# One scaling moved to GpSimd, a TensorE order pinned, and a product unit split: an FFT mixer and MLP kernel on one core

## Chip, core, metric

The kernel runs on one core of one Trainium2 chip. The metric is device time in microseconds (us), the median of several runs; smaller is better. A trace of one execution covers the span from the first to the last instruction.

## The reference, cut to what matters

```python
h  = x + irfft2(rfft2(layernorm(x)) * (w_r + 1j * w_i))     # x: [2048, 512]
h2 = h + (gelu(layernorm(layernorm(h)).T @ w1 + b1) @ w2 + b2).T   # w1: [2048, 1376]
```

## The kernel before

Both Fourier transforms are written as matrix products. The kernel has five stages:

1. Front: for each of 16 input tiles, a variance (`bn`, `ag`; for tile 3, sums on ScalarE), its inverse root (`rs`), and a Fourier matrix scaled by it (`fs`). TensorE multiplies tile and scaled matrix (`f1`), and a copy (`ys`) takes the product out of PSUM (`ps` in the traces, the output of every matmul there).
2. Middle, for eight units of four groups: forward products (`f2`), their copy (`cs`), cross products (`x`), the multiply with the filter weights on VectorE (`v`; two ops of 1024 elements for the first unit, one of 2048 for each of the next six, called large below, and two of 1024 for the last, unit 7), inverse products (`g1`), their copy (`pq`).
3. Inverse transform (`g2`, `g3`), residual, second normalisation.
4. and 5. The two layers of the MLP.

Warming matmuls multiply zeros, to keep TensorE busy; experiment 11 shows what its pace does with fewer of them: with 4 at the start, the three behind the first products took 1.46 us in the trace, and with 9, in two traces of the kernel before, 1.46 and 0.82. A scheduler in Python gives each engine its static order from modelled times; lists force parts of it. The lists that the change and the argument touch:

```python
FS_ENG = {0: "act", 3: "act", 7: "act", 9: "dve", 11: "dve", ...}     # all others: GpSimd
FRONT = {
    "act": """rs_0 fs_0 rs_1 s1_3 s2_3 rs_2 rs_3 fs_3 rs_4 ys_0 rs_5 ys_1 ys_3 rs_6 ys_2 fs_7 ...""",
    "pool": """fs_1 bv_3 fs_2 fs_4 fs_5 fs_6 fs_8 fs_10 fs_12""",
    "pe": """f1_0 f1_1 f1_3 f1_2 f1_4 ...""", ...
}
WARM_AFTER = (3, 2, 0, 1, 1, ...)      # warming matmuls (of zeros) behind f1_0, f1_1, ...
V_SPLIT = (7,)                         # unit 7's multiply in two ops
G1_WARM = {(7, 1): 2}                  # two warming matmuls before the last two groups of unit 7
...
# bv_3: a small op on GpSimd; rs_3 on ScalarE takes its result as bias
act(f"rs_{i}", RS[:, i:i + 1], V1[:, i:i + 1], ACT.Abs_reciprocal_sqrt, 1, ..., bias=BV[:, i:i + 1], ...)
```

## Time and profile before

| | |
|---|---|
| time, median of the first 3 runs | 131.5 us (131.47 to 131.62) |
| span of the first profile | 131.3 us, mean granted clock 0.987 |
| time of the very run that was profiled | 133.1 us |
| busy: TensorE, VectorE, ScalarE, GpSimd | 123.3, 70.4, 63.0, 10.8 us |

The page's lines that carry the argument are in the prediction.

### The profile page before, as it was taken

How to read it: one execution, taken by the hardware profiler on the slowest of the kernel's cores; microseconds unless marked ns; L12 is line 12 of the kernel's file. 1: busy time of each engine (PE TensorE's matmuls, PEld its weight loads, DVE VectorE, ACT ScalarE, POOL GpSimd, SP SyncE). 2: the span in 40 equal slices, each digit the busy share in tenths (PEclk: the TensorE clock that was granted, in tenths of full speed). 3: DMA queues.
4: the chain of work that ended last, by engine and by line, in shares of the span. 5: the costliest groups of instructions: out<-in, count | busy, mean ns of one | idle time of the engine just before them, and what ended most of it. 6: DMA issues, size and time to landing. Idle time of an engine off the chain costs nothing.

```text
span 131.3 us, 2029 instructions
## 1 busy us (share of the span) xinstructions
PE 123.3 (94%) x784; PEld 74.8 (57%) x784; DVE 70.4 (54%) x131; ACT 63.0 (48%) x144; POOL 10.8 (8%) x30
## 2 busy tenths in 40 slices
PE   6589989999988989999999999999999999999992
PEld 2134756787866745544444444456666666666681
DVE  0399686999992899999992000000242242332431
ACT  4098996788885999976669922222000000000000
POOL 0067850002100000000000000000000000000000
PEclk9968999999999999999999999999999999999999
DMA  3999999999999999991000000000111211112112
GB/s 72 340 419 380 290 272 293 298 280 279 410 423 419 409 408 409 416 242 42 0 0 0 0 0 0 0 0 5 40 40 40 80 40 66 57 42 80 40 42 81
DMA packets 17481, 22.17 MB, mean 169 GB/s; under 512 B 2784, under 2 KB 13408, under 8 KB 17472
## 3 DMA queue, kind: packets, MB, share of 16 engines
q1 hardware_dynamic: 17184, 21.52, 48.3%
q10 hardware_dynamic: 288, 0.52, 1.6%
q8 instruction: 6, 0.10, 0.3%
q14 instruction: 3, 0.02, 0.1%
HBM read 19.95 MB, written 2.10 MB: 168 GB/s over the span
## 4 chain that ended last, share of the span: by engine, by line
PE 75%; DVE 10%; ACT 8%; DMA 3%; issue 1%
PE ps L556 75%; DVE st L681 5%; DMA X<-in_A_x_dram 3%; DVE V L826 3%; ACT Y L574 3%; ACT EO L574 2%; ACT JK L574 1%; ACT rs L574 1%; DVE Y L743 1%; ACT PQ L574 1%; DVE mv L682 1%; PE ps L647 0%; DVE OUT L934 0%; DVE FS L659 0%; ACT FS L574 0%
## 5 line engine op out<-in xcount | busy, mean ns | idle before, releaser
L556 PE MATMUL ps<-HH,W 128*128 128x512 bf16 (+1 forms) x176 | 40.5, 379 | 0.0
L556 PE MATMUL ps<-GT,W 128*128 128x512 bf16 (+3 forms) x187 | 38.3, 367 | 0.0
L934 DVE SCALAR_TENSOR_TENSOR OUT<-ps,B2f,H 128x512 bf16<-128x512 f32 (+1 forms) x17 | 12.2, 719 | 46.3 <-PE ps L556 46.3
L556 PEld LDWEIGHTS ps<-GT,W 128*128 128x128 bf16 (+1 forms) x187 | 26.3, 145 | 12.0
L556 PEld LDWEIGHTS ps<-HH,W 128*128 128x128 bf16 (+1 forms) x176 | 17.4, 100 | 19.4 <-issue 0.6
L826 DVE TENSOR_TENSOR V<-ps,W 128x2048 bf16<-128x2048 f32 (+1 forms) x8 | 15.8, 2020 | 0.3
L574 ACT ACTIVATE JK<-H,nm 128x512 bf16<-128x512 bf16 x16 | 11.6, 725 | 3.9 <-DVE H L901 3.7
L574 ACT ACTIVATE GT<-ps,B1f 128x512 bf16<-128x512 f32 (+1 forms) x11 | 7.0, 692 | 12.7 <-PE ps L556 12.7
L681 DVE BATCH_NORM_STATS2 st<-X 128x6 f32<-128x512 bf16 x15 | 9.8, 665 | 4.2 <-DMA X<-in_A_x_dram 4.2
L901 DVE TENSOR_TENSOR H<-ps,TT 128x512 bf16<-128x512 f32 x16 | 10.9, 684 | 0.1
L647 PE MATMUL ps<-ZT 128*128 128x512 bf16 x21 | 8.0, 500 | 3.1 <-DVE st L681 1.4
L574 ACT ACTIVATE PQ<-ps 128x512 bf16<-128x512 f32 (+1 forms) x16 | 9.2, 588 | 3.6 <-PE ps L556 3.5
L556 PE MATMUL ps<-EM,V 128*128 128x128 bf16 x128 | 9.8, 219 | 0.4 <-ACT PQ L574 0.3
L574 ACT ACTIVATE EO<-ps 128x512 bf16<-128x512 f32 x16 | 9.3, 599 | 0.9 <-PE ps L556 0.9
L556 PE MATMUL ps<-FS,X 128*128 128x256 bf16 x64 | 9.0, 288 | 0.7 <-ACT FS L574 0.5
L574 ACT ACTIVATE CS<-ps 128x512 bf16<-128x512 f32 (+1 forms) x16 | 8.9, 588 | 1.2 <-PE ps L556 1.2
L556 PEld LDWEIGHTS ps<-EM,V 128*128 128x128 bf16 x128 | 7.9, 98 | 2.3 <-issue 1.1
L556 PE MATMUL ps<-EM,Y 128*128 128x256 bf16 x64 | 8.8, 273 | 0.4 <-DVE Y L743 0.4
L556 PE MATMUL ps<-EM,PQ 128*128 128x256 bf16 x64 | 8.6, 273 | 0.5 <-ACT PQ L574 0.5
L574 ACT ACTIVATE Y<-ps 128x512 bf16<-128x512 f32 (+1 forms) x15 | 8.1, 566 | 0.8 <-PE ps L556 0.8
L556 PEld LDWEIGHTS ps<-FS,X 128*128 128x128 bf16 x64 | 6.1, 102 | 3.7 <-ACT FS L574 1.0
L659 POOL TENSOR_SCALAR FS<-FP,rs 128x256 bf16<-128x256 bf16 x8 | 7.5, 940 | 8.1 <-ACT rs L574 7.9
(38 smaller groups left out, 78.5 us busy)
## 6 DMA issues: line engine op xcount, KB each, us to landing
W<-in_B_w_dram SPq DMA_DIRECT2D x8, 688.0 KB, 9.8
W<-in_B_w_dram SPq DMA_DIRECT2D x10, 512.0 KB, 16.7
out_dram<-OUT SPq DMA_DIRECT2D x15, 128.0 KB, 1.7
W<-in_A_w_r_dram SPq DMA_DIRECT2D x4, 257.0 KB, 4.8
W<-in_A_w_i_dram SPq DMA_DIRECT2D x4, 257.0 KB, 5.5
X<-in_A_x_dram SPq DMA_DIRECT2D x4, 256.0 KB, 5.4
X<-in_A_x_dram SPq DMA_DIRECT2D x2, 512.0 KB, 6.7
W<-in_A_w_r_dram SPq DMA_DIRECT2D x4, 192.8 KB, 3.5
```

Of the source, the lines that this page charges most:

```text
L556: return K.op(name, "pe", lambda eng, bank: eng.matmul(outf(bank), lhsT, rhs, start=start, stop=stop), ins=ins or [lhsT, rhs], occ=occ, la ...
L574: return eng.activation(dst, s, func, **kw)
L647: return K.op(name, "pe", lambda eng, bank: eng.matmul(ps[:, bank, :], ZT[:, 0:NP], ZT[:, :], start=True, stop=True), ins=[ZT[:, :]], occ= ...
L659: dve(f"fs_{i}", lambda eng, bank: eng.tensor_scalar(FS[:, i, :, :], FP[:, i, :, :], rs, None, op0=ALU.mult), [FP[:, i, :, :], rs], [FS[:, ...
L681: dve(f"bn_{i}", lambda eng, bank, i=i, x=x: eng.bn_stats(ST[:, i, 0:6], x), [x], [ST[:, i, 0:6]], 512, prio=25)
L682: dve(f"ag_{i}", lambda eng, bank, i=i: eng.bn_aggr(MV[:, i, :], ST[:, i, 0:6]), [ST[:, i, 0:6]], [MV[:, i, :]], 20, prio=32)
L743: dve(name, lambda eng, bank: eng.tensor_copy(dst, src(bank)), [], [dst], n, unit=unit, prio=28, last=last)
L826: return eng.tensor_tensor(vout, s, win, ALU.mult)
L901: return eng.tensor_tensor(hs.rearrange("p (h d) -> p h d", h=2), e, tt[:, :, :], ALU.add)
L934: dve(f"fin{s2}_{c0}", lambda eng, bank, dst=dst, bia=bia, hs=hs, n=c1 - c0: eng.scalar_tensor_tensor(dst, ps[:, bank, 0:n], bia, hs, op0= ...
```

## The change

Its intent: relieve ScalarE, the busiest engine of the second part of the front (7.24 of 7.40 us), of one scaling; pin a TensorE order that helps VectorE's chain of multiplies to start; and shorten what stands between VectorE's last multiply and the inverse transform.

```diff
-FS_ENG = {0: "act", 3: "act", 7: "act", ...
+FS_ENG = {3: "act", 7: "act", ...
-    "act": """rs_0 fs_0 rs_1 s1_3 s2_3 rs_2 rs_3 ...
+    "act": """rs_0 s1_3 rs_1 s2_3 rs_2 rs_3 ...
-    "pool": """fs_1 bv_3 fs_2 ...
+    "pool": """fs_0 fs_1 bv_3 fs_2 ...
-V_SPLIT = (7,)
+V_PARTS = {7: ((0, 2), (2, 1), (3, 1))}       # unit 7 in ops of 2, 1 and 1 groups
-G1_WARM = {(7, 1): 2}
+G1_WARM = {(7, 1): 1}
+def fill_order():        # the order of f2 and x at the entry, forced on TensorE
+    ...
+    return f2(0) + f2(1) + f2(2)[:3] + x(0) + f2(2)[3:] + f2(3) + x(1) + [n for g in range(4, 16) for n in f2(g)]
 ...                      # the code that emits v_7 takes its parts from V_PARTS
```

More of the change, by code (lines that the diff above doesn't have):

```diff
@@ L496 @@
 RS_GROUPS = ((0,), (1,), (2,), (4,), (5,), (6, 7), (8,), (9, 10), (11, 12), (13,), (14, 15))
-FS_ENG = {0: "act", 3: "act", 7: "act", 9: "dve", 11: "dve", 13: "dve", 14: "dve", 15: "dve"}
+FS_ENG = {3: "act", 7: "act", 9: "dve", 11: "dve", 13: "dve", 14: "dve", 15: "dve"}
 Y_EVAC = (("single", ("act",), ("act",)),) * 6 + (("single", ("dve",), ("act",)), ("single", ("dve",), ("act", "act")))
@@ L502 @@
         tl_0 th_0 h_0 tl_1 th_1 h_1 hh_0""",
-    "act": """rs_0 fs_0 rs_1 s1_3 s2_3 rs_2 rs_3 fs_3 rs_4 ys_0 rs_5 ys_1 ys_3 rs_6 ys_2 fs_7 rs_8 ys_4 ys_5 rs_9 ys_7 rs_11 ys_6 ys_8
+    "act": """rs_0 s1_3 rs_1 s2_3 rs_2 rs_3 fs_3 rs_4 ys_0 rs_5 ys_1 ys_3 rs_6 ys_2 fs_7 rs_8 ys_4 ys_5 rs_9 ys_7 rs_11 ys_6 ys_8
         rs_13 ys_9 ys_10 rs_14 ys_11 ys_13 yh_150 yh_151
         eo_0 eo_1 eo_2 eo_3 eo_4 q_0 r2_0 eo_5""",
-    "pool": """fs_1 bv_3 fs_2 fs_4 fs_5 fs_6 fs_8 fs_10 fs_12""",
+    "pool": """fs_0 fs_1 bv_3 fs_2 fs_4 fs_5 fs_6 fs_8 fs_10 fs_12""",
     "pe": """f1_0 f1_1 f1_3 f1_2 f1_4 f1_5 f1_7 f1_6 f1_8 f1_9 f1_10 f1_11 f1_12 f1_13 f1_14 f1_15""",
@@ L511, with f2, x @@
 WARM_AFTER = (3, 2, 0, 1, 1, 0, 0, 1, 0, 0, 0, 0, 0, 0, 0, 0)
-V_SPLIT = (7,)
+V_PARTS = {7: ((0, 2), (2, 1), (3, 1))}
 LAST_WARM = 7
 MM1B_FROM = {5: 54000.0, 6: 62000.0}
-G1_WARM = {(7, 1): 2}
+G1_WARM = {(7, 1): 1}
+def fill_order():
+    def f2(g):
+        return [f"f2_{g}_{k}" for k in (("00", "10", "01", "11") if g == 0 else ("00", "01", "10", "11"))]
+    def x(g):
+        return [f"x_{g}_{c}{r}" for c in range(2) for r in range(2)]
+    return f2(0) + f2(1) + f2(2)[:3] + x(0) + f2(2)[3:] + f2(3) + x(1) + [n for g in range(4, 16) for n in f2(g)]
 def build_kernel(nc, A_x, A_w_r, A_w_i, B_w1, B_b1, B_w2, B_b2, out):
@@ L525, in build_kernel @@
     K.forced = {e: FRONT[e].split() for e in ("dve", "act", "pool")}
-    K.forced["pe"] = [f"{n}_{b}{h}" for n in FRONT["pe"].split() for b in range(2) for h in "ab"]
+    K.forced["pe"] = [f"{n}_{b}{h}" for n in FRONT["pe"].split() for b in range(2) for h in "ab"] + fill_order()
     T = K.setup_memory(memory_layout(), es)
@@ L815, in stage_x, with tt @@
         g0 = 4 * u
-        nh = 2 if u in V_SPLIT else 1
-        ng = 4 // nh
-        for h in range(nh):
-            wt = W[:, g0 + h * ng:g0 + h * ng + ng, :, :]
+        for gl, ng in V_PARTS.get(u, ((0, 4),)):
+            wt = W[:, g0 + gl:g0 + gl + ng, :, :]
             win = bass.AP(wt.tensor, wt.offset + 1, [list(wt.ap[0]), [LW, 2 * ng], [1, 2], [2, NP]])
-            vout = V[:, g0 + h * ng:g0 + h * ng + ng, :, :].rearrange("p g w l -> p (g w l)")
-            def tt(eng, bank, h=h, win=win, vout=vout):
-                s = psf[:, bank * 512 + h * 512:bank * 512 + h * 512 + 256 * ng]
+            vout = V[:, g0 + gl:g0 + gl + ng, :, :].rearrange("p g w l -> p (g w l)")
+            def tt(eng, bank, gl=gl, ng=ng, win=win, vout=vout):
+                s = psf[:, bank * 512 + gl * 256:bank * 512 + gl * 256 + 256 * ng]
                 s = bass.AP(s.tensor, s.offset, [list(s.ap[0]), [256, ng], [0, 2], [1, 256]])
                 return eng.tensor_tensor(vout, s, win, ALU.mult)
-            K.op(f"v_{u}_{h}", "dve", tt, ins=[wt], outs=[vout], occ=50.0 + 2130.0 / nh, lat=170.0 + 2130.0 / nh, unit=unit, pr=True,
-                 last=h == nh - 1, prio=11, after=wload[u])
+            K.op(f"v_{u}_{gl}", "dve", tt, ins=[wt], outs=[vout], occ=50.0 + 532.5 * ng, lat=170.0 + 532.5 * ng, unit=unit, pr=True,
+                 last=gl + ng == 4, prio=11, after=wload[u])
     lastg1 = [None]
```

## The prediction

> **What bounds the kernel now.** I read the windows view first, cut where the work changes: 5.3 to 12.2 us (statistics and first products), to 19.6 (rest of the forward transform), to 23.9 (entry of the middle stage), to 39.9 (middle stage), to 41.2 (its exit), to 47.8 (inverse transform and second normalisation), then both layers of the MLP. Columns: stretch, length, busy us and instruction count of TensorE, weight load, VectorE, ScalarE and GpSimd, granted clock, DMA share, GB/s.
>
> ```profile
> 5.30:12.20 6.90, 5.46 (x24) 2.33 (x25) 6.80 (x20) 5.21 (x16) 4.00 (x5) 0.75 1.03 406
> 12.20:19.60 7.40, 6.63 (x51) 4.41 (x52) 5.84 (x19) 7.24 (x20) 5.20 (x12) 1.00 1.10 286
> 19.60:23.90 4.30, 4.29 (x44) 2.90 (x45) 2.78 (x3) 2.71 (x6) 0.00 (x0) 1.00 1.08 294
> 23.90:39.90 16.00, 15.47 (x209) 12.29 (x206) 15.81 (x8) 13.37 (x26) 1.28 (x7) 1.00 1.05 343
> 39.90:41.20 1.30, 0.82 (x11) 0.53 (x9) 0.44 (x2) 0.65 (x2) 0.00 (x0) 1.00 1.06 436
> 47.80:131.30 83.50, 80.94 (x396) 46.78 (x396) 33.77 (x70) 26.58 (x63) 0.00 (x0) 1.00 0.22 76
> ```
>
> The reader is to see a different limit in each row: ScalarE from 12.2 to 19.6 us (7.24 of 7.40), VectorE's eight large multiplies from 23.9 to 39.9 (15.81 of 16.00), and from 47.8 on TensorE, which nothing in the change touches. The change can only bring the start of the inverse transform (41.2 us) forward or put it back, and what it gains there arrives nearly whole at the end.
>
> Second, the timeline of the first stage (start, length, engine, line, operation, count, idle before and who ended it):
>
> ```profile
> 6.60 0.51 ACT L574 ACTIVATE FS<-FP,rs 128x256 bf16<-128x256 bf16 x1
> 7.17 0.87 PE L556 MATMUL ps<-FS,X 128*128 128x256 bf16 x4 [0.48 <-ACT FS L574]
> 7.46 0.93 POOL L659 TENSOR_SCALAR FS<-FP,rs 128x256 bf16<-128x256 bf16 x1 [6.62 <-ACT rs L574]
> 8.10 1.46 PE L647 MATMUL ps<-ZT 128*128 128x512 bf16 x3
> 9.35 1.06 PE L556 MATMUL ps<-FS,X 128*128 128x256 bf16 x4
> 10.47 0.74 PE L647 MATMUL ps<-ZT 128*128 128x512 bf16 x2
> 11.05 1.04 PE L556 MATMUL ps<-FS,X 128*128 128x256 bf16 x8
> 11.69 0.60 ACT L574 ACTIVATE Y<-ps 128x512 bf16<-128x512 f32 x1 [0.64 <-PE ps L556]
> 14.72 0.29 DVE L659 TENSOR_SCALAR FS<-FP,rs 128x256 bf16<-128x256 bf16 x1 [1.17 <-ACT rs L574]
> ```
>
> TensorE stands in one unbroken queue from the first scaled matrix (7.17 us) to the third product (11.05 us), warming matmuls between; ScalarE waits 0.64 us for that product, and from there it hardly stops until 18.2 us. VectorE then waits 1.17 us for ScalarE's ninth statistic. So the first scaling, done at 7.11 us, looks critical by way of TensorE's queue, though the chain of waits itself runs through VectorE's statistics at this place.
>
> Third, the timeline of VectorE in the middle and of the exit:
>
> ```profile
> 21.43 2.36 DVE L811 TENSOR_TENSOR V<-ps,W 128x1024 bf16<-128x1024 f32 x2 [0.76 <-PE ps L556]
> 23.93 2.29 DVE L826 TENSOR_TENSOR V<-ps,W 128x2048 bf16<-128x2048 f32 x1
> ...
> 39.68 0.59 PE L647 MATMUL ps<-ZT 128*128 128x512 bf16 x2
> 40.11 0.61 PE L556 MATMUL ps<-EM,V 128*128 128x128 bf16 x8
> 40.54 0.42 DVE L857 CAST PQ<-ps 128x256 bf16<-128x256 f32 x1 [0.62 <-PE ps L556]
> 40.76 0.38 ACT L574 ACTIVATE PQ<-ps 128x256 bf16<-128x256 f32 x1 [0.59 <-PE ps L556]
> 41.20 0.39 PE L556 MATMUL ps<-EM,PQ 128*128 128x256 bf16 x2 [0.48 <-ACT PQ L574]
> ```
>
> The first two multiplies end at 23.79 us and the next starts at 23.93; and at the exit two warming matmuls stand in front of the last eight products, although their last input was ready at 39.91 us.
>
> [...] granted clock 0.50 from 7.38 to 10.78 us (TensorE busy only 1.49 of the 3.40 us before), and 1.00 afterwards. [...] the trace shows 1.22 us at 1024 and 2.28 at 2048 elements[...], so I use it for 512: 0.69 us, an estimate. [...] the 128x256 scaling takes 0.93 us on GpSimd, 0.28 on VectorE and 0.51 on ScalarE. [...]
>
> **The change, part by part.**
>
> First scaling on GpSimd. ScalarE loses one instruction of 0.51 us, some 0.40 of its pace. GpSimd is idle, and would start 0.09 us after the statistic ends at 6.57 (the gap before its scaling at 7.46 in the trace), end at 7.59, and hand over in some 0.08: the first product at 7.67 instead of 7.17, 0.50 later. Behind it the queue is serial. With the clock at half until 10.79 as now: four products 1.06 (the row at 9.35), handover 0.06, three warming matmuls 1.25 (8.10 to 9.35), four products 1.0, handover 0.05, two warming matmuls now at full clock 0.44. Sum 7.67 + 3.86 = 11.5 against 11.05: the third product is some 0.44 late, and so are its copy on ScalarE and all behind it. The 0.40 us that ScalarE saves lie before its wait of 0.64 us, so they only lengthen that wait. What speaks against charging all of it: the clock's switch may move in favour of the later start, and there is relief in the order of ScalarE's early statistics. I charge +0.25, a choice between 0.05 and 0.44.
>
> TensorE order at the entry. As traced the order is already the one now fixed, but for one product: the fourth of group 3 stands behind the four of the second cross unit (it starts at 22.09, they at 21.77). Fixed, it starts at some 21.67; its copy on ScalarE starts right after the one before, at 22.06 instead of 22.41, and the cross products of the next unit, held by that copy until 23.18, could start at 22.75, when the first multiply has freed their bank. The third multiply then starts when VectorE is free, about 23.71 instead of 23.93: −0.22. The whole VectorE chain has four such holes, 0.22, 0.13, 0.15 and 0.12 (starts against the pace of 2.20 us for 2048 elements), 0.62 together; the later three lie behind an order that the change doesn't fix, so I count none of them.
>
> Last unit in three ops, one warming matmul fewer. VectorE's last op of 1024 elements (1.21 us) becomes two of 0.69 that overlap by 0.08: it ends at 39.99 instead of 39.91, so +0.08 there. But the four products of the third quarter need only the first of them (39.38) and start behind the single warming matmul, at 39.68 + 0.22 = 39.90 instead of 40.11; the last four follow at 40.12, their input being there. Last product of the stage: 40.50 instead of 40.72; the copy and the inverse transform follow: −0.21.
>
> Later stages: nothing is edited there, but the order is chosen from modelled times, so it may come out otherwise. TensorE's only holes there are some 0.20 at 46.6 and 0.49 at 47.8 us: ±0.3, mean 0.
>
> Sum: +0.25 − 0.22 − 0.21 = −0.18, so 131.5 − 0.2 = **131.3 us**.
>
> **The rivals.** The first: the front pays the full +0.44, because TensorE's queue there really is serial. For it: ScalarE's wait of 0.64 us named TensorE, and no idle time of 0.1 us on ScalarE behind it. Then 131.5, and up to 131.9 if the middle gives its gain back. The second: the front hides the later start altogether, because another input holds the third product or the clock comes up in time; for it, that the chain of waits names VectorE's statistics up to 12.17 us; against, that VectorE sits idle 1.17 us afterwards. Then 131.5 − 0.43 = 131.1, and 130.7 if the new order closes the other holes of VectorE. The third: the multiply that starts earlier becomes bound by TensorE (its next cross products ended at 26.21, 0.06 before the multiply that needs them), so that the 0.22 is lost one unit later and the gain is the exit's alone: 131.5 + 0.25 − 0.21 = 131.5.
>
> **Range and chances.** The rivals span 130.7 to 131.9, and 2% is 2.6 us, more than all holes named. I take 130.7 to 131.8 for 8 in 10, and faster 0.02, same 0.97, slower 0.01.
>
> **What would show it right or wrong.** In the changed profile: the first product near 7.7, the third near 11.3 to 11.5 and the first product of the middle stage between 19.6 and 20.1 us; the first 2048-element multiply no more than 0.05 us after the one before ends; from the last multiply's end to the inverse transform 1.0 us instead of 1.29; and from there to the end the same 90.1 us. Wrong if the third product comes no later (then the front was not bound by that queue), if the middle grows holes elsewhere, or if the last stretch changes by over 0.3 us.

The marks stand where statements on the clock, on the time of a multiply and on GpSimd's rate were cut, which no trace of this case shows; the traced figures beside them remain. No term of the sum is cut: +0.25 − 0.22 − 0.21 = −0.18. The 0.69 us for 512 elements had been worked out with a formula; a straight line through the two traced times gives the same, 1.22 − (2.28 − 1.22)/2 = 0.69, an estimate. That the clock comes up earlier or later was a guess; the traces show only that its time differs: full clock is recorded from 10.79 us on in the first profile and from 9.61 in that of experiment 11, and in the second profile of before three warming matmuls take 0.82 us from 7.18 on, against 1.46 in the stretch at 0.50. The handover from GpSimd to TensorE, put at some 0.08 us, was 0.06 in the changed kernel's trace (6.94 to 7.00).

## The result

The changed kernel takes 131.65 us (131.60 to 131.73, 4 runs), the kernel before 131.55 us in the same rounds. The ratio is 1.0009, with a 95% interval from 0.9991 to 1.0026: the same, if anything 0.1 us slower. A ratio here and below is the mean time of one kernel's fast runs over that of the other's of the same rounds, so not quite the ratio of the medians quoted.

The profile of the changed kernel has a span of 129.9 us and a clock of 1.00. Against the first profile of before (131.3 us) this looks like a gain of 1.4 us, which the times deny. So before was profiled again, unchanged, in the first experiment: 129.8 us and 1.00. In both of these traces the first statistic starts at 4.67 us, so they can be laid side by side. The windows view was cut, in each kernel, at the first statistic, the first product of the middle, the first multiply, the first multiply of unit 7, the first product of the inverse transform, and the end. The columns are as in the prediction.

Kernel before, profiled again:

```profile
4.67:18.11 13.44, 11.16 (x76) 6.38 (x76) 12.65 (x37) 12.26 (x34) 9.18 (x17) 1.00 1.05 345
18.11:19.93 1.82, 1.82 (x17) 1.28 (x18) 0.43 (x2) 1.02 (x3) 0.00 (x0) 1.00 1.01 271
19.93:36.05 16.12, 16.05 (x209) 12.41 (x207) 15.82 (x8) 13.38 (x26) 1.28 (x7) 1.00 1.08 322
36.05:39.70 3.65, 2.50 (x34) 2.02 (x35) 2.78 (x3) 2.32 (x5) 0.00 (x0) 1.00 1.02 418
39.70:129.79 90.09, 86.59 (x435) 51.19 (x443) 38.49 (x81) 32.37 (x76) 0.00 (x0) 1.00 0.29 106
```

Changed kernel:

```profile
4.67:18.38 13.71, 11.03 (x75) 6.36 (x75) 12.64 (x37) 11.89 (x33) 10.06 (x18) 1.00 1.07 344
18.38:20.20 1.82, 1.82 (x17) 1.28 (x18) 0.43 (x1) 1.02 (x3) 0.00 (x0) 1.00 1.08 275
20.20:36.33 16.13, 16.05 (x209) 12.34 (x207) 15.82 (x8) 13.38 (x26) 1.27 (x7) 1.00 1.06 312
36.33:39.76 3.43, 2.50 (x33) 1.92 (x34) 2.84 (x4) 2.31 (x5) 0.00 (x0) 1.00 1.03 427
39.76:129.86 90.10, 87.18 (x443) 51.26 (x443) 38.50 (x81) 32.35 (x76) 0.00 (x0) 1.00 0.29 107
```

The second number of each row is the stretch's length. The front is 0.27 us longer, the entry and the middle are level, the exit is 0.22 us shorter, and the rest is level. The sum is about +0.06 us, which agrees with the +0.1 us of the times. Differences of 0.1 us in the first and the last stretch are no chance: in the nine traces that have the scaling on ScalarE (the first profile and that of experiment 11 left out) the front takes 13.43 or 13.44 us, and from the inverse transform to the end all fourteen traces take 90.08 to 90.15 us. (The 435 and 443 matmuls of the last row are no change: the first profile of before has 443 as well, in the same order as the changed kernel; some records are missing.)

Where the front lost its 0.27 us is seen in the timeline between the first statistic and the statistic of tile 3. Before, profiled again (ScalarE's second statistic, GpSimd's second scaling, GpSimd's bias op, ScalarE's statistic of tile 3):

```profile
6.41 0.30 ACT L574 ACTIVATE rs<-mv,eps 128x1 f32<-128x1 f32 x1
...
6.80 0.93 POOL L659 TENSOR_SCALAR FS<-FP,rs 128x256 bf16<-128x256 bf16 x1 [5.96 <-ACT rs L574]
...
7.72 0.31 POOL L667 TENSOR_SCALAR bv<-sm 128x1 f32<-128x1 f32 x1
...
8.13 0.29 ACT L574 ACTIVATE rs<-v,bv 128x1 f32<-128x1 f32 x1
```

Changed (GpSimd's first and second scaling merged into one line, ScalarE's sum of tile 3, its second statistic, the bias op, the statistic of tile 3):

```profile
6.01 2.01 POOL L668 TENSOR_SCALAR FS<-FP,rs 128x256 bf16<-128x256 bf16 x2 [5.17 <-ACT rs L583]
6.08 0.63 ACT L583 ACTIVATE JK<-X 128x512 bf16<-128x512 bf16 x1 [0.17 <-DMA X<-in_A_x_dram]
...
6.71 0.28 ACT L583 ACTIVATE rs<-mv,eps 128x1 f32<-128x1 f32 x1
...
7.99 0.32 POOL L676 TENSOR_SCALAR bv<-sm 128x1 f32<-128x1 f32 x1
...
8.41 0.29 ACT L583 ACTIVATE rs<-v,bv 128x1 f32<-128x1 f32 x1 [0.45 <-POOL bv L676]
```

GpSimd's two scalings end at 8.02 instead of 7.73, so the bias op starts at 7.99 instead of 7.72. ScalarE now stands idle 0.45 us for it, and takes up the statistic of tile 3 at 8.41 instead of 8.13. This is the 0.28 us: from there to the copy of the third product ScalarE shows no idle time in either kernel, and each instruction of it is late by the same amount. GpSimd's second scaling is late for two reasons. It queues behind the first one (6.01 + 0.93 = 6.94, 0.14 later than its old start at 6.80). And its input, the second statistic, ends at 6.99 instead of 6.71, because the sum ahead of it waited for its tile and took 0.63 us.

In the middle, VectorE's timeline before (profiled again), the six multiplies of 2048 elements and the two of unit 7 as one merged line:

```profile
22.43 15.98 DVE L826 TENSOR_TENSOR V<-ps,W 128x2048 bf16<-128x2048 f32 x8
```

and changed:

```profile
20.20 2.36 DVE L820 TENSOR_TENSOR V<-ps,W 128x1024 bf16<-128x1024 f32 x2 [0.76 <-PE ps L565]
22.59 2.29 DVE L833 TENSOR_TENSOR V<-ps,W 128x2048 bf16<-128x2048 f32 x1
25.05 13.70 DVE L833 TENSOR_TENSOR V<-ps,W 128x2048 bf16<-128x2048 f32 x8 [0.17 <-PE ps L565]
```

In the changed kernel the first of the large ones starts 0.03 us after the two before it end (22.56), as the pinned order wanted. But the next one waits 0.17 us for TensorE. Counted from the first multiply, it starts 4.85 us later in the changed kernel (25.05 − 20.20) and 4.84 us later in the one before (24.77 − 19.93, from the unmerged trace). The gain at the first is lost at the second.

At the exit of the changed kernel, the last eight inverse products, their two copies:

```profile
38.68 0.61 PE L565 MATMUL ps<-EM,V 128*128 128x128 bf16 x8
39.10 0.42 DVE L864 CAST PQ<-ps 128x256 bf16<-128x256 f32 x1 [0.34 <-PE ps L565]
39.32 0.38 ACT L583 ACTIVATE PQ<-ps 128x256 bf16<-128x256 f32 x1 [0.38 <-PE ps L565]
```

They start 2.35 us after the first multiply of unit 7 (36.33), against 2.56 in the kernel before (profiled again), whose first multiply of unit 7 starts at 36.05:

```profile
38.61 0.61 PE L556 MATMUL ps<-EM,V 128*128 128x128 bf16 x8
```

### The profile page after: what moved, and what is told of

Its sections match the earlier page's. It is cut to its first block, busy times and chain, and to the rows that moved or that the text cites. A ratio compares the mean times of both kernels' runs of the same rounds, so it can differ in the third digit from the quotient of the medians.

```text
span 129.9 us, 2029 instructions
## 1 busy us (share of the span) xinstructions
PE 122.1 (94%) x783; PEld 74.3 (57%) x783; DVE 70.5 (54%) x132; ACT 62.4 (48%) x143; POOL 11.6 (9%) x31
## 4 chain that ended last, share of the span: by engine, by line
PE 76%; DVE 10%; ACT 8%; DMA 3%; issue 1%
PE ps L565 76%; DVE st L690 4%; DVE V L833 3%; DMA X<-in_A_x_dram 3%; ACT Y L583 3%; ACT EO L583 2%; ACT JK L583 1%; ACT rs L583 1%; DVE Y L752 1%; ACT PQ L583 1%; DVE mv L691 1%; DVE OUT L941 0%; DVE FS L668 0%; ACT FS L583 0%; PE ps L656 0%
## 5 line engine op out<-in xcount | busy, mean ns | idle before, releaser
L833 DVE TENSOR_TENSOR V<-ps,W 128x2048 bf16<-128x2048 f32 (+2 forms) x9 | 15.9, 1811 | 0.3 <-PE ps L565 0.2
L656 PE MATMUL ps<-ZT 128*128 128x512 bf16 x20 | 7.2, 470 | 2.3 <-DVE ZT L603 1.2
L668 POOL TENSOR_SCALAR FS<-FP,rs 128x256 bf16<-128x256 bf16 x9 | 8.4, 935 | 6.0 <-ACT rs L583 5.7
```

The lines of the kernel that those rows point to most:

```text
L656: return K.op(name, "pe", lambda eng, bank: eng.matmul(ps[:, bank, :], ZT[:, 0:NP], ZT[:, :], start=True, stop=True), ins=[ZT[:, :]], occ= ...
L668: dve(f"fs_{i}", lambda eng, bank: eng.tensor_scalar(FS[:, i, :, :], FP[:, i, :, :], rs, None, op0=ALU.mult), [FP[:, i, :, :], rs], [FS[:, ...
L833: return eng.tensor_tensor(vout, s, win, ALU.mult)
```

## The experiments

There were twelve runs, one of the kernel before and eleven of edited kernels, all with correct results. Unless said otherwise each was timed in five rounds against the kernel before.

### 1. The kernel before, profiled again

No edit; the question is the state of the first profile.

> The kernel before, unchanged, profiled again. Theory A: the first profile of before (span 131.3 us, clock 0.987, its own time 133.1 us) fell in an execution with a half-clock window that the timed runs (131.5 us) do not have; then the new profile has clock 1.00 and a span of 129.8 +- 0.2 us, 1.8 us under the time as in the four runs of the changed kernel (129.9 under 131.65), and its first scaled product starts about 1.85 us after the first statistic starts. Rival B: the half-clock window belongs to the kernel before; then clock 0.987 and 131.3 us again. Time ratio 1.000 in both.

It took 131.58 us against 131.60 (ratio 1.0001, 0.9989 to 1.0013), with a span of 129.8 us and a clock of 1.00. The first scaled product started 1.84 us after the first statistic. Theory A holds: the first profile was of a slower execution. Compared to this one, in the first profile the first statistic is 0.66 us later (5.33 against 4.67) and the first product of the middle another 0.84 us later after it (14.28 against 13.44), with half clock in between (0.50 from 7.38 to 10.78 us); 0.66 + 0.84 is the whole 1.5 us.

### 2. The scaling on GpSimd alone

```diff
 # kernel before
-FS_ENG = {0: "act", 3: "act", ...          +FS_ENG = {3: "act", ...
-"act": rs_0 fs_0 rs_1 s1_3 s2_3 ...        +"act": rs_0 s1_3 rs_1 s2_3 ...
-"pool": fs_1 bv_3 fs_2 ...                 +"pool": fs_0 fs_1 bv_3 fs_2 ...
```

> The kernel before with the first scaling moved to GpSimd and nothing else. Theory A (the scaling holds GpSimd 0.93 us, so GpSimd's second scaling and the small bias op behind it come late, ScalarE's third statistic waits for that op, and ScalarE is busy without a break from there): +0.3 us, 131.85. Rival B (the front hides it, and the changed kernel is level because middle and exit gave nothing): +-0.05 us, 131.55.

It took 131.91 us against 131.60 (ratio 1.0035, 1.0011 to 1.0060). One of its six runs, at 132.98 us with a clock of 0.987, is in the ratio; the other five lie from 131.81 to 131.96. Theory A holds. In its trace ScalarE waits 0.32 us for the bias op; the statistic of tile 3 starts 3.60 us after the first statistic, against 3.46 before and 3.74 in the changed kernel. It is only 0.14 late here because the input tile of ScalarE's sum had landed earlier relative to the first statistic (1.25 us after it, against 1.39 in the trace of the changed kernel), so that ScalarE's second statistic was done just when GpSimd came free of its first scaling: here GpSimd's own queue accounts for the whole delay, and the later statistic adds nothing to it. The front of this trace is 0.14 us longer than before (13.58 against 13.44 us), not 0.31; how the 0.31 us of the median comes about in the other runs stays open. No run has the scaling on GpSimd with ScalarE's old order of `rs_1` and `s1_3`, so the two edits of this step are told apart by the traces alone.

### 3. The changed kernel with the scaling back on ScalarE

```diff
 # changed kernel: the three lines of experiment 2, reversed
```

> The changed kernel with the first scaling back on ScalarE; TensorE order, three-op unit and single warming matmul stay. Theory A: -0.2 us against before, 131.35, about 0.3 under the changed kernel. Rival B: as the changed kernel, 131.65.

131.35 us against 131.60 (ratio 0.9985, 0.9973 to 0.9997). In its trace the front takes 13.44 us, as before, and the whole from the first statistic on 124.90 us, against 125.12 before and 125.19 in the changed kernel. The rest of the change is worth 0.2 us, and the scaling lost it.

### 4. The bias op first

```diff
 # changed kernel
-"pool": fs_0 fs_1 bv_3 fs_2 ...
+"pool": fs_0 bv_3 fs_1 fs_2 ...
```

> The changed kernel, GpSimd's small bias op put in front of its second scaling (order: first scaling, bias op, second scaling). Theory A (the late bias op is the cost): ScalarE's statistic of tile 3 starts some 0.25 us earlier, 131.35 to 131.4. Rival C (the late first product on TensorE's queue is the cost, as predicted): the first product is as late as in the changed kernel and the time stays at 131.65.

The median is 131.38 us against 131.60. One of six runs took 132.88 us; with it the ratio is 0.9999 (0.9966 to 1.0033), which alone says nothing. The other five lie from 131.19 to 131.40, under ten of before's eleven (131.37 to 131.80). The trace decides between the theories. The bias op, the statistic of tile 3 and the third product (the first four of these eight):

```profile
6.94 0.31 POOL L676 TENSOR_SCALAR bv<-sm 128x1 f32<-128x1 f32 x1
7.77 0.28 ACT L583 ACTIVATE rs<-v,bv 128x1 f32<-128x1 f32 x1
9.33 1.04 PE L565 MATMUL ps<-FS,X 128*128 128x256 bf16 x8
```

The first statistic starts at 4.53 us in this trace. The third product on TensorE starts 4.80 us after the first statistic, even later than in the changed kernel (4.76) and 0.45 later than before. Yet the statistic of tile 3 starts after 3.24 us, and the first product of the middle after 13.36, 0.35 earlier than in the changed kernel and 0.08 earlier than before. So the late bias op cost the time and the late products did not.

But of these 0.35 us only 0.15 reaches the end: from the first statistic on the whole takes 125.04 us, against 125.19 in the changed kernel and 124.90 in experiment 3. In this trace the last of the filter weights landed at 29.43 us, and the fourth large multiply, ready at about 28.96, started at 29.45.

### 5. The exit alone

```diff
 # kernel before
-V_SPLIT = (7,)              +V_PARTS = {7: ((0, 2), (2, 1), (3, 1))}
-G1_WARM = {(7, 1): 2}       +G1_WARM = {(7, 1): 1}
```

> The kernel before with only the exit changed (last unit in three ops, one warming matmul fewer). Theory A (the whole gain is the exit's, the TensorE order gives nothing because the next multiply waits for its own cross products instead): the same as with the order kept, -0.22 us against before, 131.35; in the trace, from the first multiply's start to the inverse transform 19.56 us instead of 19.77. Rival D (the order gives 0.1 to 0.2 of it): 131.45 to 131.55.

131.39 us against 131.57 (ratio 0.9984, 0.9971 to 0.9998). Experiment 3, which has the pinned order as well, had 0.9985. In the traces both take the same 124.90 us from the first statistic to the end. The pinned order, as the change has it, is worth nothing, and experiment 2 plus this one (+0.31 − 0.18) makes +0.13 us, near the +0.10 of the whole change.

### 6 and 7. The two exit edits apart

```diff
 # kernel of experiment 3; run 6                # run 7
-G1_WARM = {(7, 1): 1}                          -V_PARTS = {7: ((0, 2), (2, 1), (3, 1))}
+G1_WARM = {(7, 1): 2}                          +V_PARTS = {7: ((0, 2), (2, 2))}
```

> The changed kernel with the first scaling back on ScalarE and with two warming matmuls at the exit as before; the last unit stays in three ops. Theory A (the two exit edits are worth something only together: the second warming matmul pushes the last eight products back by 0.22 us, whatever the split): level with before, 131.6. Rival F (the split alone is the gain): 131.35.

> The changed kernel with the first scaling back on ScalarE and the last unit in two ops as before; one warming matmul. Theory A: the last eight products then wait for the second op's end, 0.07 us before their start with two warming matmuls: 0.05 to 0.1 us under before, 131.5. Rival G (the missing warming matmul alone is the gain): 131.35.

Three ops with two warming matmuls: 131.73 us against 131.57 (ratio 1.0008, 0.9995 to 1.0020). Two ops with one: 131.44 (0.9986, 0.9974 to 0.9999). The cleaner measure is the stretch from the first multiply of unit 7 to the inverse transform: 3.64 us before (3.65 above, where the edges were rounded), 3.63 with the split alone, 3.50 with one warming matmul alone, 3.43 with both. The split alone gives nothing, as expected: the second warming matmul covers it. The missing matmul alone gives 0.14, twice what was expected; I had taken a longer handover from VectorE to TensorE than the 0.05 us that the trace shows there. The split adds its 0.07 only then.

In both of these traces the fourth large multiply was held by the filter weights. VectorE's timeline of run 7, from the fourth multiply on:

```profile
29.60 8.95 DVE L833 TENSOR_TENSOR V<-ps,W 128x2048 bf16<-128x2048 f32 x5 [0.35 <-DMA W<-in_A_w_i_dram]
```

The weights landed at 29.58 us here, and at 28.35 us in the second profile of before, where the multiply was ready at 29.18. So with a faster front or middle this load is the next bound, in some executions and not in others.

### 8. The order pinned one step further

```diff
 # kernel of experiment 3
-... + x(1) + [n for g in range(4, 16) for n in f2(g)]
+... + x(1) + f2(4) + f2(5)[:3] + x(2) + x(3) + f2(5)[3:] + g1(0..3) + x(4) + x(5) + [n for g in range(6, 16) for n in f2(g)]
```

> The changed kernel with the first scaling back on ScalarE, and TensorE's order fixed one step further: the last product of forward group 5 ahead of the first inverse products, and the cross products of the third unit ahead of forward groups 6 and 7. Theory A (the third multiply's cross products end 0.2 us too late, which ate what the fixed order gave): the hole in front of the second 2048-element multiply closes and the chain ends 0.2 us earlier, 131.15. Rival E (VectorE's chain is then held further on, by the last block of filter weights landing at 28.9 us or later, or by later cross products): 131.35.

A miss: 132.36 us against 131.57 (ratio 1.0055, 1.0042 to 1.0069). The hole that it aimed at did close: the second large multiply started 19.85 us after the first statistic instead of 20.11. But a new hole of 1.08 us stands in front of the sixth, waiting for TensorE. The scheduler, fed with other modelled times, had put the cross products of that unit behind inverse and forward products.

### 9. TensorE's whole middle order written out

```diff
 # kernel of experiment 3
-+ fill_order()
++ MID      # the order of experiment 3 as a list, with: f2_5_11 behind x_3; x_4, x_5 ahead of f2_6, f2_7;
+           # f2_10_11, f2_12_11 with their groups; g1_15_11, g1_19_11 ahead of x_10, x_12
```

> As the run with the order fixed further, but with TensorE's whole order of the middle stage written out, so that nothing later is rearranged: that of the changed kernel with the last product of forward groups 5, 10 and 12 kept with its group, the third unit's cross products ahead of forward groups 6 and 7, and the last inverse product of units 3 and 4 ahead of the cross products. Theory A (VectorE's holes are TensorE's order): the holes before the second, fifth and seventh large multiply close, 0.25 + 0.15 + 0.13: 130.9 with scaling on ScalarE, and exit as changed. Theory A with rival E (the fourth multiply cannot start before the last filter weights land, 28.4 to 29.6 us in the runs so far): some 0.25 of that is lost in front of the fourth, 131.1. Rival: 131.35, nothing.

131.29 us against 131.68 (ratio 0.9966, 0.9954 to 0.9978). This is the fastest kernel, faster than before by some 0.4 us and than the changed one. Its runs and those of the changed kernel were not in the same rounds; by their ratios to before it takes 0.9957 of the changed kernel's time (0.9966 / 1.0009). VectorE's timeline from the first large multiply on:

```profile
22.37 8.89 DVE L851 TENSOR_TENSOR V<-ps,W 128x2048 bf16<-128x2048 f32 x4
31.64 6.82 DVE L851 TENSOR_TENSOR V<-ps,W 128x2048 bf16<-128x2048 f32 x5 [0.38 <-PE ps L583]
```

The first four now run without a break, but the fifth waits 0.38 us. In the trace the gain over experiment 3 is therefore only 0.08 us (124.82 against 124.90 from the first statistic to the end). How much of the 0.4 us in the times is more than that and the exit's 0.22 is not settled; the intervals are as wide as the difference.

### 10. The filter weights in halves

```diff
 # kernel of experiment 9
-for ch, (u0, u1) in enumerate(((0, 1), (1, 4), (4, 8))):
+for ch, (u0, u1) in enumerate(((0, 1), (1, 4), (4, 6), (6, 8))):
```

> The previous kernel, with the last block of filter weights (units 4 to 7) loaded as two blocks (4 and 5, 6 and 7), each with its own wait: eight more transfers of half the size. Rival E holds if the fourth multiply then starts right behind the third and the time falls 0.1 to 0.3 us below the previous kernel, 130.85 to 131.0. If the weights are not what holds it: the same time; if the extra issues (0.65 us each) delay the later loads: slower.

In the first profile four issues of such a weight block took 2.60 us, 0.65 each.

131.52 us, against 131.29 for experiment 9 in the same rounds (ratio to before 0.9977, 0.9962 to 0.9992). It is inconclusive as a test: in neither trace was the fourth multiply held, and both take 124.82 us from the first statistic to the end. The fourth multiply started right behind the third at 29.33 us while the last weights landed only at 30.82, so it no longer waited for the whole load; but nothing shows what this is worth in an execution where the undivided load would be late. Nor is the last rival of the expectation excluded, that the added transfers cost time: the median is 0.23 us worse, though the intervals of the two ratios overlap.

### 11. Fewer warming matmuls at the start

Timed in three rounds.

```diff
 # kernel before
-N_WARM = 9
+N_WARM = 4
```

> The kernel before with 4 instead of 9 warming matmuls at the very start[...]. Theory A (the 1.2 to 1.6 us by which the first profile of before was longer than its timed runs are one half-clock window over the first products): every run has a mean clock of 0.98 to 0.99, the third product is some 1.4 us later after the first statistic, 132.8 to 133.1 us. Rival: the long profile was long for its late inputs alone (0.66 us later) and the clock costs nothing: 131.6.

The mark stands for a length of time that TensorE would have to be busy; no run shows such a length, and it is cut.

132.95 us against 131.68 (ratio 1.0087, 1.0058 to 1.0116; runs from 132.30 to 133.43). TensorE's timeline, the three warming matmuls behind the first products:

```profile
8.11 1.46 PE L647 MATMUL ps<-ZT 128*128 128x512 bf16 x3
```

The three take 1.46 us, as in the first profile of before, and 0.82 in the second one (start at 7.18). In the first profile the clock is recorded at 0.50 over these three, so the same pace is taken for half clock here. The third product starts 1.06 us later after the first statistic (5.41 against 4.35), and the first product of the middle 0.54 us later (13.98 against 13.44). The other 0.51 us of this trace's longer span are a later first statistic (5.18 against 4.67). ScalarE waits 0.43 us for the third product here, a wait that apart from this trace only the first profile of before shows (0.64 us). The rival, that the clock costs nothing, falls; of theory A the cause holds and the size does not. Read so, the clock costs 0.5 us here, not 1.2 to 1.6. And the mean granted clock reads 1.00, though the pace shows half: the clock's record in this trace has its first entry at 9.61 us, and what went before is counted as full (1.00 for 5.0 to 9.6 us in the windows view, the three matmuls in it). The 1.27 us by which the median is longer is thus explained for 0.5 us only; whether the later input is chance, and why the times of this kernel spread over 1.1 us, is not settled.

### 12. Cross products further ahead

```diff
 # kernel of experiment 9: in MID, x_10 and x_11 ahead of g1_14; x_12 and x_13 ahead of g1_18
```

> The kernel with the pinned TensorE order, with the cross products of units 5 and 6 moved ahead of eight inverse products each. Theory A: there the hole of 0.38 us in front of the fifth large multiply came from cross products that ended at 31.57 us, 0.4 us after VectorE was free; moved ahead they end at about 31.1 and the hole closes: 0.3 to 0.4 us under the pinned kernel, 0.75 us under before, 130.9. Rival: a later multiply waits for its cross products, or for a copy on ScalarE, instead: level with the pinned kernel, 0.4 us under before.

131.89 us against 131.76 (ratio 1.0005, 0.9961 to 1.0048); a run of 132.83, and two such of before, make the interval wide. The rival's mechanism holds, and it costs more than the rival said. The fifth large multiply now starts without a hole, 26.46 us after the first statistic instead of 26.92. But the inverse products put back delay their copy on ScalarE, this delays the last forward copies, and the multiply of unit 7 waits 0.54 us for its cross products. From the first statistic to the end it is 125.16 us, against 124.82 in experiment 9, so 0.34 us worse where the rival said level.

## Why the prediction was right, and where its steps were not

The time of 131.65 us lies in the range of 130.7 to 131.8, and "same" had 0.97 of the chances. That is little merit: 2% is 2.6 us, and the range was wide enough to hold both a gain and a loss. The sum, −0.18, should have been about +0.1, so the sign was wrong, and its steps fared differently.

**What bounds the kernel now.** That gains and losses before the inverse transform arrive at the end held: 90.09 and 90.10 us in the two traces. But the front was read from an execution in half clock, in which TensorE's queue stood in front of ScalarE. The two traces of the kernel before differ in it: the clock is 0.50 from 7.38 to 10.78 us in the first and full there in the second. I quoted the fall and did not ask whether the timed runs have it, although the 133.1 us of the profiled run were there to be read.

**First scaling on GpSimd, charged +0.25 by way of TensorE's queue.** The size came out right (0.27 in the changed kernel's trace; in experiment 2 0.31 in the times and 0.14 in its trace), the mechanism was not, so the size was luck. The third product did come later, by 0.41 us counted from the first statistic (4.76 against 4.35), as the working said (0.44 there, though its own terms add up to 11.53 us, 0.48 late). But in the usual state it is not what ScalarE waits for. The 0.28 us arise from the bias op that stands behind two scalings in GpSimd's queue, and experiment 4 shows it: with the bias op ahead the products are later still and the front is faster than before. The step "they only lengthen that wait" failed, as there is no such wait in the usual state. The prediction's signs could not tell: it took a third product that comes later as a sign of being right, and the product did come later, but nothing waited for it. The second rival, that the front hides the scaling altogether, is refuted by experiment 2.

**TensorE order at the entry, −0.22.** The pinned order moved the first large multiply, though by 0.11 us only (17.65 against 17.76 us after the first statistic, experiments 3 and 1): its cross products now came through TensorE's own queue, behind the forward products of groups 4 and 5, and not at once when the bank was free. What failed is the assumption that the chain behind it follows. The third rival described what happens: the second multiply's cross products were then the last to come, and experiments 3 and 5 show the order to be worth nothing. I had written this rival down, with its number of 0.06 us, and still put the full −0.22 in the sum.

**Last unit in three ops, one warming matmul fewer, −0.21.** This step was right in mechanism and size: 0.22 in the trace, 0.18 in experiment 5. By experiments 6 and 7, 0.14 of it comes with the single warming matmul alone, and the split adds the rest. The estimate of 0.69 us for the 512-element op, which lies on the straight line through the traced 1.22 us at 1024 and 2.28 at 2048 elements, was met by 0.68.

**Later stages, ±0.3.** Nothing was rearranged there, and the length did not change (90.09 and 90.10 us).

**The second rival's best case**, with VectorE's holes closed by the order, was reached only in part by experiment 9. Experiments 8 and 12 show why: each closed hole opened another one further on.

## What to carry to other kernels

Before a profile is read, compare the time of the very run that it shows with the times that are to be explained; if they differ by more than the effect in question, profile again. When work moves to an idle engine, look at what is queued behind it there: a 0.3 us op on which another engine waits can cost more than the move saves (here ScalarE waited 0.45 us for it, and the front grew by 0.27 us although ScalarE had lost an op of 0.51). And a static order tuned to within 0.1 us is tuned in all its places at once, so that closing one hole counts only after the next wait has been checked.

## What the runs showed beside this

- The execution in half clock is not peculiar to the kernel before: a run of experiment 2 (132.98 us) had the clock of 0.987 as well. Not every slow run shows it: one of experiment 4 took 132.88 us at a mean clock of 1.00, which, after experiment 11, does not exclude half clock at the start.
- A start at the pace of half clock is the rule here, and the mean clock does not show it: it reads 0.998 to 1.000 in thirteen of the fourteen traces (1.00 in experiment 11, where three matmuls of 512 columns took 1.46 us instead of 0.82), while in all fourteen traces the first warming matmuls start 0.43 us apart, as in the half-clock stretch of the first profile, and from the first entry of the clock's record on (between 3.8 and 9.6 us) 0.22 us apart.
- The first profile is the one trace in which the clock fell again during the front. In its first recorded stretch of 3.41 us TensorE was busy for 1.50 us, and the stretch of half clock followed; in the first 3.41 us of the record of the others, where the clock stayed up, it was busy longer, least of all for 1.75 (experiment 10), 1.76 (changed kernel) and 1.80 us (experiment 3). This is one fall, so no threshold is shown.
- The first input tile landed between 4.5 and 5.3 us in the traces, and this alone moves the span by more than any part of the change.
- Half clock, in experiment 11 read from the pace, lengthened the front by 0.54 us (experiment 11) and 0.84 us (first profile of before) of some 130.
- The same 128x256 bf16 scaling took 0.93 us on GpSimd, 0.51 on ScalarE and 0.28 on VectorE (first profile).
- The last filter weights, loaded as one block, landed between 28.35 us (experiment 1) and 29.58 us (run 7), which decided whether a multiply waited (0.35 us in run 7).
